# Forty-one unread products of the identity among the opening's instructions on TensorE

## The chip, the cores and the metric

One NeuronCore of a Trainium2 chip runs the kernel. The metric is device time in microseconds (us), from three runs of the kernel before: 505.88, 505.97 and 508.54, median 505.97. Lower is better.

TensorE multiplies and transposes (PE in the profile, its weight loads PEld), VectorE (DVE) and ScalarE (ACT) do elementwise work and read TensorE's results out of the accumulation memory PSUM, GpSimd (POOL) does elementwise work and issues transfers, SyncE (SP) only issues transfers. Each engine runs its own instructions strictly in the order of the program; semaphores hold one engine back until another has delivered.

## What is computed

Two layers in fp32. The first is a delta-rule attention with a state of 48 x 48 for each of 4 x 8 heads, over 768 steps:

```python
k_n = k / (np.linalg.norm(k, axis=-1, keepdims=True) + 1e-06)
state = np.zeros((B, H, D, D))
for t in range(S):
    y[:, :, t] = einsum('bhd,bhde->bhe', q[:, :, t], state)
    v_old = einsum('bhde,bhd->bhe', state, kt)
    state = state + bt[..., None, None] * einsum('bhd,bhe->bhde', kt, vt - v_old)
```

The second takes its output as 3072 tokens of 384 numbers and applies a maxout network, with w1, w2 and w3 of 384 x 768 and w_out of 768 x 384:

```python
h = np.maximum(np.maximum(x @ w1, x @ w2), x @ w3)
return h @ w_out
```

## The kernel before

**Tiling.** The 768 steps are cut into 12 chunks of 64. A chunk has two units, one for each pair of batch entries, so there are 24 units. Two chunks (512 tokens) form a group, and there are six groups. Inside a chunk the recurrence is turned into matrix products. That needs the Gram matrices of keys with keys and keys with queries, and the inverse of a triangular matrix for each head. The inverse is found by forward substitution on VectorE (`solve`, from line 507), all heads at once. Then small products on TensorE join the halves of the inverse and make the updates `u`, the outputs `y` and the state `st`.

**Order.** The whole order is written out by hand, under a manual schedule: the program's order is each engine's order. The last part of the kernel (from line 1276) is this order. First comes the opening, straight-line code for the first chunks; then the six groups of the second layer, `ffn(0)` to `ffn(5)`, with the recurrence of the next group laid between their products.

**The opening, line by line of what TensorE gets.** `turn(n, (0,))` transposes unit n's keys by four products with the identity (tile `p_t`, line 338) and copies them out; `turn(n, (1,))` does the same for queries. `keys(n)` and `gram(n, ...)` make Gram matrices (`p_g`, line 415) and copy them out (lines 426 and 432). `some(solving, n)` issues n steps of the forward substitution on VectorE (lines 561 and 565). At the end of group 0's substitution the result is transposed on VectorE (line 573) and placed in `ut` by copies of VectorE and ScalarE (line 505). Next, for chunk 0, come `halves_z` (`p_e`, line 685), `halves_u` (`p_f`, line 696), `join_z` (`p_z`, line 713), `join_u` (`p_j`, line 726), `new` (`p_u`, line 771), `to_y` (`p_y`, line 813) and `to_x` (`p_x`, line 832). Each is a batch of 32 small products, in two halves where it is chunk 0, and a copy follows on ScalarE or VectorE that the next batch needs. `to_x` is six transposes, which fill the tile `xt` that the second layer reads.

Between them stand `some(conv, 1)`, one step of the conversion of the second layer's weights (three instructions on ScalarE, lines 247 to 249, one on VectorE, line 259, one on GpSimd, line 263), and `fetch`, which loads a piece of them. `solve(1)` starts the second group's inverse; its substitution runs on VectorE in the stretch after the opening.

`ffn(0)` then starts with products `p_h` (line 1224) of `xt` with converted weights. Between its first steps lie, in this order, chunk 1's `halves_z`, chunk 0's state update (`p_s`, line 794, added to `st` on VectorE at line 801), chunk 1's `halves_u`, and `old_k` (`p_k`, line 743, subtracted from `v_t` on VectorE at line 755).

**The product in question.** `busy(n, of)` at line 1290 already exists. It multiplies the 128 x 128 identity by `of`, n times, into a PSUM tile `p_w` that nothing reads. The tile takes one of the two slots named `ffn`, which in the opening nothing else uses. Before, it is called once, at line 1309, ahead of the first transposes of keys. A product in fp32 is two matmul instructions in the trace; a transpose is one.

Of the kernel before, what the change touches and what calls it, by code (L numbers as in the profile page):

```python
# [23 lines left out]
def kernel(  # L24
# [76 lines left out]
    ident = const.tile([128, 128], FP32, name="ident")  # L101
# [208 lines left out]
    def first_norms():  # L310
        nc.vector.transpose(out=nrm_0.rearrange("p c g h -> p (c g h)"), in_=bl_0[0])
# [7 lines left out]
    def by_par(t):  # L319
        return t.rearrange("p (j two) x -> p two j x", two=2)  # L320

    def turn(n, parts=(0, 1), copy=nc.scalar.copy):

        if n not in kqts:
            if n == 6:
                kqts[n] = work.tile([128, KT, TOK], FP32, name="xt").rearrange(
                    "p k t -> p (k t)"
                )[:, 0 : NP * 4 * C].rearrange(
                    "p (j b i t) -> p j b i t", b=2, i=2, t=C
                )  # L330
            else:
                kqts[n] = work.tile([128, NP, 2, 2, C], FP32, name="kqt", bufs=6)
        kqt = kqts[n]
        p_t = ps_two("p_t")
        for i in parts:
            src = (kpad[place(n)], qpad[n % NQ])[i]
            for j in range(NP):
                nc.tensor.transpose(
                    p_t[:, i, j * 128 : (j + 1) * 128],
                    src[:, 2 * j : 2 * j + 2],  # L340
                    ident,
                )
        some = slice(parts[0], parts[-1] + 1)
        copy(  # L344
            kqt.rearrange("p j b i t -> p i (j b) t")[:, some],
            p_t.rearrange("p i (x t) -> p i x t", t=C)[:, some],
        )
# [50 lines left out]
    def masked(t, of, engine=nc.vector):  # L398
        engine.tensor_tensor(  # L399
            out=by_par(t), in0=of,  # L400
            in1=mask[:, None, None, :].to_broadcast([128, 2, NP, C]), op=ALU.mult,
        )

    def gram(n, parts=(0, 1), queues=one_queue, copy=nc.scalar.copy, later=False):
        kqt, g = kqts[n], n % 2
        p_g = ps_two("p_g")

        whole = len(parts) == 2 and not g
        for j in range(NP):
            for par in range(2):  # L410
                for bb in range(2):
                    kq = kqt[dims(par), j, bb ^ g]
                    for i in (0,) if whole else parts:
                        c0 = j * 128 + i * C
                        nc.tensor.matmul(  # L415
                            p_g[
                                rows(bb ^ (g * i)), par, c0 : c0 + C * (1 + whole)
                            ],
                            kq[:, 0],
                            kq if whole else kq[:, i],  # L420
                        )
        p_v = p_g.rearrange("p two (j i t) -> p two j i t", j=NP, i=2)
        if 1 in parts:
            pt = pts[n] = square("pt")
            if later:
                copy(by_par(pt), p_v[:, :, :, 1])
            else:
                masked(pt, p_v[:, :, :, 1])
        if 0 not in parts:
            return  # L430
        at = ats[n] = square("at")
        copy(by_par(at), p_v[:, :, :, 0])  # L432
        if queues:
            to_dram(n, queues)
# [192 lines left out]
    def turn_t1(c):  # L627

        t, u_t = t1[c % NU], ut[c % NU]
        nc.vector.transpose(out=t[:, 0], in_=u_t[:, 0, :, 0:BL])  # L630
        for bb in range(2):
            nc.vector.transpose(
                out=t[block(1 - bb), 1], in_=u_t[block(bb), 1, :, 0:BL]
            )
# [41 lines left out]
    def halves_z(c):  # L676
        if c > 1:
            halves_t(c)
        at = [ats[2 * c + g] for g in range(2)]
        second = ut[c % NU].rearrange("p g h (f two x) -> p g h f two x", two=2, x=HB)  # L680
        for hs, p_v, copy in heads_of(c, "p_e", BL):
            for i, h in enumerate(hs):
                for bb, g in TILES:
                    r = rows(bb)
                    nc.tensor.matmul(
                        p_v[rows(bb ^ g), g, i], at[g][r, h], second[r, g, h, :, 1]
                    )
            copy(zs[c % NU][:, :, span(hs)], p_v)

    def halves_u(c):  # L690
        t, z = fine.pop(c), zs[c % NU]
        for hs, p_v, negate in negated_of(c, "p_f", BL):
            for i, h in enumerate(hs):
                for bb, g in TILES:
                    r = rows(bb ^ g)
                    nc.tensor.matmul(p_v[bb][rows(bb), g, i], t[g][r, h], z[r, g, h])
            for f in (0, 1):
                for bb in range(2):
                    r = block(bb, f, HB)
                    negate[bb](  # L700
                        ut[c % NU][r, :, span(hs), BL * f + HB : BL * (f + 1)],
                        p_v[bb][r, :, :, HB * f : HB * (f + 1)],
                        -1.0,
                    )

    def join_z(c):
        at = [ats.pop(2 * c + g) for g in range(2)]
        z, second = zs[c % NU], ut[c % NU][:, :, :, BL:C]
        for hs, p_v, _ in heads_of(c, "p_z", BL):
            for i, h in enumerate(hs):  # L710
                for bb, g in TILES:
                    r = block(bb, 1)
                    nc.tensor.matmul(
                        p_v[block(bb ^ g), g, i], at[g][r, h, 0:BL], second[r, g, h]
                    )
            for bb in range(2):
                nc.scalar.copy(z[block(bb), :, span(hs)], p_v[block(bb)])

    def join_u(c):
        z, t = zs[c % NU], t1[c % NU]  # L720
        u12 = ut[c % NU][:, :, :, BL:C]
        for hs, p_v, negate in negated_of(c, "p_j", BL):
            for i, h in enumerate(hs):
                for bb, g in TILES:
                    r = block(bb ^ g)
                    nc.tensor.matmul(p_v[bb][block(bb), g, i], t[r, g, h], z[r, g, h])  # L726
            for bb in range(2):
                negate[bb](u12[block(bb), :, span(hs)], p_v[bb][block(bb)], -1.0)
# [36 lines left out]
    def new(c):  # L765
        rhs = rhss.pop(c)
        u = us[c] = both("u", D, 2)
        for hs, p_v, copy in heads_of(c, "p_u", D):
            for i, h in enumerate(hs):
                for bb, g in TILES:  # L770
                    nc.tensor.matmul(  # L771
                        p_v[rows(bb ^ g), g, i],
                        ut[c % NU][rows(bb), g, h],
                        rhs[rows(bb), g, h],
                    )
            copy(u[:, :, span(hs)], p_v)
        if c + NU < 2 * FINE:
            for bb in range(2):
                corner = ut[c % NU][block(bb), :, :, BL:C]
                zero = kpad[0][block(bb), None, 0:1, D : D + 1]  # L780
                nc.scalar.copy(corner, zero.to_broadcast(corner.shape))
# [494 lines left out]
    def some(gen, n):  # L1276
        for _ in range(n):
            if next(gen, gen) is gen:
                break
# [10 lines left out]
    def busy(n, of):  # L1290
        p_w = ps_ffn([128, TOK], "p_w")[:, 0 : of.shape[1]]
        for _ in range(n):
            nc.tensor.matmul(p_w, ident, of)

    def keys(n, queues=one_queue, copy=nc.scalar.copy):
        gram(n, (0,), queues, copy)
# [30 lines left out]
    some(solving, 1)  # L1327
    keys(4)
    keys(5)
    turn(6, (0,))  # L1330
    turn(0, (1,))
    load_q(3, (nc.gpsimd, nc.gpsimd))
    load_beta()
    keys(6)
    gram(0, (1,), None, later=True)
    turn(7, (0,))
    turn(1, (1,))
    keys(7)
    turn(2, (1,))
    gram(1, (1,), None, later=True)  # L1340
    turn(3, (1,))
    some(conv, 1)
    gram(2, (1,), None, later=True)
    gram(3, (1,), None, later=True)
    some(solving, HB + 1)
    halves_t(0)
    halves_z(0)
    first_norms()
    some(conv, 1)
    placed(1, 0)  # L1350
# [3 lines left out]
    for _ in range(2):  # L1354
        fetch(nc.gpsimd)
    halves_u(0)
    turn_t1(0)
    join_z(0)
    masked(pts[0], by_par(pts[0]))
    placed(1, 2)  # L1360
    join_u(0)
    masked(pts[1], by_par(pts[1]))
    old_k(0)
    old_q(0)
    new(0)
    some(conv, 1)
    fetch(nc.gpsimd)
    load_v(1, nc.gpsimd)
    placed(1, 3)
    to_y(0)  # L1370
    halves_t(1)
    solving = solve(1)
    some(solving, 1)
    to_x(0)
    some(conv, 1)


# [177 lines left out]
```

## Time and profile before

| view | value |
|---|---|
| median of three runs | 505.97 us (505.88 to 508.54) |
| the profiled execution's span | 505.2 us |
| TensorE busy | 484.0 us, 96% of the span |
| VectorE busy | 361.1 us, 71% |
| ScalarE busy | 169.4 us, 34% |
| GpSimd busy | 187.1 us, 37% |
| mean granted TensorE clock | 0.968 |

The span runs from the first instruction to the last in one profiled execution. Busy time is the sum of recorded instruction times; matmuls are pipelined, so consecutive records overlap and a busy TensorE is not one at its peak. The granted clock is given as a share of full speed: 1.00 is full, 0.50 is half. A wait shows as idle time before an instruction, with the instruction that ended it.

### The profile page before, as it was taken

Reading aid. Unit: us, or ns where it says so; the run is one execution under the profiler, and the core shown is the slowest. Engines: PE = TensorE matmul, PEld = TensorE weight load, DVE = VectorE, ACT = ScalarE, POOL = GpSimd, SP = SyncE. Lnnn points to the kernel's source line nnn. Section 1 sums busy time; section 2 is a strip of 40 time slices with the busy share of each in tenths; the row PEclk is TensorE's granted clock in tenths of the full one; section 3 lists DMA queues with packets and bytes.
Section 4 is the critical chain, followed back from the end, with each engine's and each line's share of the span. In section 5 each row is a group of like instructions: output and inputs, shape, how many; then the busy total and the mean of one; then the engine's idle time right before and its main releaser. Section 6 shows DMA issues by size and latency. Waiting matters only on the chain.

```text
span 505.2 us, 18676 instructions
## 1 busy us (share of the span) xinstructions
PE 484.0 (96%) x8064; PEld 338.0 (67%) x8064; DVE 361.1 (71%) x835; ACT 169.4 (34%) x320; POOL 187.1 (37%) x311
## 2 busy tenths in 40 slices
PE   7678989999999999999999999999999999999996
PEld 6467767855566555565565565555797457998895
DVE  5888799787996441799652999565998874468753
ACT  5585664885422142210152200242201032212210
POOL 7434472793391935770395880501000020000000
PEclk9855899999999999999999999999999999999999
DMA  8937869864045934544584652744224230340002
GB/s 114 205 50 214 195 142 160 198 181 137 3 120 134 191 72 77 146 119 117 112 156 104 158 137 74 149 72 96 64 54 90 47 86 15 85 94 1 0 18 47
DMA packets 109121, 53.50 MB, mean 106 GB/s; under 512 B 92208, under 2 KB 102864, under 8 KB 109040
## 3 DMA queue, kind: packets, MB, share of 16 engines
q1 hardware_dynamic: 97280, 31.78, 31.0%
q0 software_dynamic: 9216, 19.85, 16.5%
q8 instruction: 63, 1.03, 0.9%
q10 hardware_dynamic: 2544, 0.69, 0.8%
q14 instruction: 18, 0.15, 0.1%
HBM read 39.17 MB, written 13.11 MB: 103 GB/s over the span
## 4 chain that ended last, share of the span: by engine, by line
PE 76%; DVE 11%; ACT 4%; DMA 3%; SPq 3%; issue 2%; POOL 0%; DVEq 0%; ACTq 0%; POOLq 0%
PE p_h L1224 28%; PE p_o L985 13%; PE p_o L1262 12%; PE p_c L1163 5%; DVE tmp L561 3%; PE p_g L415 2%; PE p_m L905 2%; PE p_u L771 2%; PE p_k L743 2%; DVE y_p L565 2%; DMA kmore<-in_k_dram 2%; PE p_y L813 2%; PE p_s L794 2%; PE p_q L743 1%; PE p_j L726 1%
## 5 line engine op out<-in xcount | busy, mean ns | idle before, releaser
L1224 PE MATMUL p_h<-xt,w_sb 128*128 128x512 f32 (+1 forms) x450 | 186.8, 558 | 0.6 <-ACT xt L839 0.6
L1224 PEld LDWEIGHTS p_h<-xt,w_sb 128*128 128x128 f32 x450 | 82.4, 193 | 69.2 <-issue 61.6
L1238 DVE TENSOR_TENSOR h<-h,p_h 128x512 f32<-128x512 f32 (+1 forms) x42 | 25.5, 607 | 46.8 <-PE p_h L1224 46.3
L565 DVE TENSOR_TENSOR y_bl<-y_bl,tmp 128x31 f32<-128x31 f32 (+20 forms) x139 | 50.4, 363 | 4.8
L561 DVE TENSOR_TENSOR tmp<-x_bl,y_bl 128x31 f32<-128x31 f32 (+20 forms) x139 | 48.8, 351 | 3.9
L1262 PE MATMUL p_o<-wo_sb,h 128*128 128x384 f32 x144 | 48.9, 490 | 0.0
L373 POOL DMA_DIRECT2D turned<-in_q_dram x72 | 39.3, 554 | 4.6 <-POOL turned L368 3.1
L1262 PEld LDWEIGHTS p_o<-wo_sb,h 128*128 128x128 f32 x144 | 26.7, 190 | 17.2
L1234 ACT ACTIVATE h<-p_h 128x512 f32<-128x512 f32 x24 | 14.3, 597 | 69.2 <-PE p_h L1224 69.2
L263 POOL TENSOR_TENSOR w_sb<-mant,up 128x384 int32<-128x384 int32 x18 | 19.0, 1054 | 39.5 <-DVE mant L259 37.8
L415 PEld LDWEIGHTS p_g<-kqt 48*64 48x64 f32 x1216 | 24.5, 142 | 9.2 <-issue 6.3
L415 PE MATMUL p_g<-kqt 48*64 48x64 f32 (+1 forms) x1216 | 27.7, 241 | 0.9 <-ACT kqt L344 0.8
L1268 ACT COPY o_sb<-p_o 128x384 f32<-128x384 f32 x12 | 5.8, 479 | 62.6 <-PE p_o L1262 56.5
L801 DVE TENSOR_TENSOR st<-st,p_s 48x768 f32<-48x768 f32 (+1 forms) x18 | 17.1, 949 | 12.7 <-PE p_s L794 12.4
L399 DVE TENSOR_TENSOR pt<-p_g,mask 128x512 f32<-128x512 f32 x20 | 13.8, 690 | 17.0 <-PE p_g L415 16.9
L598 POOL DMA_DIRECT2D ut<-y_d x4 | 2.6, 653 | 60.6 <-DMA y_d<-y_bl 60.6
L148 POOL DMA_DIRECT2D v_t<-in_v_dram x14 | 11.6, 832 | 35.3 <-PE p_u L771 35.3
L368 POOL MEMSET turned<- 128x96 f32 x18 | 3.3, 191 | 49.4 <-DVE kqt L389 49.4
L771 PEld LDWEIGHTS p_u<-v_t,ut 64*64 64x64 f32 x768 | 13.5, 141 | 8.4 <-issue 7.3
L432 ACT COPY at<-p_g 128x512 f32<-128x512 f32 x22 | 12.8, 585 | 17.4 <-DVE pt L399 15.4
L373 POOL DMA_DIRECT2D turned<-in_k_dram x32 | 17.5, 556 | 1.2 <-POOL turned L368 1.2
L1163 PE MATMUL p_c<-xt,w_sb 128*128 128x256 f32 x72 | 17.7, 379 | 0.0
(239 smaller groups left out, 907.3 us busy)
## 6 DMA issues: line engine op xcount, KB each, us to landing
w_bits<-in_moe_w_dram SPq DMA_DIRECT2D x9, 384.0 KB, 6.2
w_bits<-in_moe_w_dram POOLq DMA_DIRECT2D x9, 384.0 KB, 5.7
turned<-in_q_dram POOLq DMA_DIRECT2D x72, 48.0 KB, 2.8
out_dram<-o_sb SPq DMA_DIRECT2D x36, 96.0 KB, 2.3
y_x<-y SPq DMA_DIRECT2D x32, 96.0 KB, 3.0
qall<-y_x SPq DMA_DIRECT2D x32, 96.0 KB, 2.8
v_t<-in_v_dram POOLq DMA_DIRECT2D x14, 192.0 KB, 5.0
at_d<-at SPq DMA_DIRECT2D x72, 32.0 KB, 3.0
```

What stands on the lines that cost most here:

```text
L263: nc.gpsimd.tensor_tensor(out=dst.bitcast(I32), in0=mant_v.bitcast(I32), in1=up_v, op=ALU.add)
L373: (queue, nc.gpsimd)[i].dma_start(out=t[p0 : p0 + 32, bb, at : at + NP * 2 * D].rearrange("p (j x) -> p j x", j=NP), in_=(k, q)[i][2 * bb ...
L415: nc.tensor.matmul(p_g[rows(bb ^ (g * i)), par, c0 : c0 + C * (1 + whole)], kq[:, 0], kq if whole else kq[:, i],)
L561: nc.vector.tensor_tensor(out=t_v, in0=row.to_broadcast(t_v.shape), in1=column.to_broadcast(t_v.shape), op=ALU.mult,)
L565: nc.vector.tensor_tensor(out=rest, in0=rest, in1=t_v, op=ALU.subtract)
L771: nc.tensor.matmul(p_v[rows(bb ^ g), g, i], ut[c % NU][rows(bb), g, h], rhs[rows(bb), g, h],)
L801: nc.vector.tensor_tensor(out=s_v[r], in0=s_v[r], in1=p_s[r, :, 0 : H * D], op=ALU.add)
L985: nc.tensor.matmul(to[:, g], a[j][:, 128 * g : 128 * (g + 1)], b[j], start=(start and g == j == 0), stop=(stop and g == 1 and j == len(a) ...
L1163: nc.tensor.matmul(to, w[stays], moves, start=(n == 0), stop=(n == len(terms) - 1))
L1224: nc.tensor.matmul(p_h, w_sb[i][:, t, f * 128 : (f + 1) * 128], xt[:, t, lo : lo + w], start=(t == 0), stop=(t == KT - 1),)
L1238: nc.vector.tensor_tensor(out=h, in0=h, in1=p_h, op=ALU.max)
L1262: nc.tensor.matmul(p_o, stays, moves, start=(n == 0), stop=(n == len(terms) - 1))
```

## The change

At twelve places of the opening a call of `busy` with the identity is put in: 2, 3, 3, 6, 6, 2, 4, 3, 4, 3, 3 and 2 products, 41 in all. Nothing is removed or moved, and no transfer is added. In the program's order these places are: before the turn of unit 6's keys; before the turn of unit 7's keys; before the queries of units 2 and 3; after the last Gram matrix of group 0, ahead of `halves_z(0)`; and after `halves_z`, `halves_u`, `join_z`, `join_u`, `new`, `to_y` and `to_x` of chunk 0.

```diff
     keys(5)
+    busy(2, ident)
     turn(6, (0,))
...
     gram(0, (1,), None, later=True)
+    busy(3, ident)
     turn(7, (0,))
     turn(1, (1,))
     keys(7)
+    busy(3, ident)
     turn(2, (1,))
     gram(1, (1,), None, later=True)
+    busy(6, ident)
     turn(3, (1,))
     some(conv, 1)
     gram(2, (1,), None, later=True)
     gram(3, (1,), None, later=True)
+    busy(6, ident)
     some(solving, HB + 1)
     halves_t(0)
     halves_z(0)
+    busy(2, ident)
     first_norms()
...
     halves_u(0)
+    busy(4, ident)
     turn_t1(0)
     join_z(0)
+    busy(3, ident)
     masked(pts[0], by_par(pts[0]))
     placed(1, 2)
     join_u(0)
+    busy(4, ident)
     masked(pts[1], by_par(pts[1]))
     old_k(0)
     old_q(0)
     new(0)
+    busy(3, ident)
...
     to_y(0)
+    busy(3, ident)
     halves_t(1)
     solving = solve(1)
     some(solving, 1)
     to_x(0)
+    busy(2, ident)
     some(conv, 1)
```

## The prediction

> **What bounds the kernel now.** I looked first at the busy time by long stretches (columns: stretch and length; busy us and instructions of PE, PEld, DVE, ACT, POOL; granted clock; DMA share; GB/s).
>
> ```profile
> 30.00:55.00 25.00, 22.51 (x618) 19.46 (x622) 19.43 (x46) 15.16 (x37) 14.00 (x15) 0.54 0.58 147
> 55.00:90.00 35.00, 31.62 (x710) 26.14 (x701) 32.05 (x83) 22.08 (x42) 15.88 (x20) 1.00 0.89 165
> 100.00:500.00 400.00, 399.85 (x6113) 267.75 (x6112) 279.10 (x639) 106.30 (x196) 134.98 (x232) 1.00 0.41 93
> ```
>
> From 100 us on TensorE never waits: what reaches that point earlier ends earlier. From 55 to 90 VectorE sets the pace (32.05 of 35 us, the substitution of `solve(1)`). Before that the clock stands at 0.54. So I cut the opening finely, along the steps at which the clock changed. Slices of 0.1 us put these at 18.97, 22.38, 25.79 and 53.07 us: steps of 3.41, 3.41 and 27.28, which is 8 times 3.41.
>
> ```profile
> 12.15:15.56 3.41, 2.17 (x72) 1.88 (x72) 2.84 (x6) 2.06 (x6) 2.21 (x3) 1.00 0.93 166
> 15.56:18.97 3.41, 2.14 (x72) 1.60 (x70) 2.77 (x11) 2.62 (x5) 1.94 (x3) 1.00 1.25 217
> 18.97:22.38 3.41, 3.41 (x56) 2.63 (x60) 3.03 (x11) 1.53 (x3) 2.27 (x5) 0.50 1.36 224
> 22.38:25.79 3.41, 0.87 (x32) 0.70 (x24) 3.02 (x12) 0.81 (x2) 0.00 (x0) 1.00 1.10 199
> 46.25:49.66 3.41, 3.41 (x76) 2.58 (x77) 3.12 (x10) 0.43 (x2) 0.00 (x0) 0.50 0.89 197
> 49.66:53.07 3.41, 3.41 (x72) 3.05 (x68) 1.47 (x4) 2.14 (x4) 3.19 (x3) 0.50 0.84 149
> ```
>
> Each clock holds for such a slot and answers to the slot before: 2.14 us of work lost it, 2.17 kept it, a full slot (3.41) won it back at 22.38, 0.87 lost it again, and from 25.79 it stayed at half until 53.07. One full slot, from 46.25, did not win it; it holds the small products `p_e` in half its length.
>
> Third, the timeline of TensorE, for what half clock costs and where it waits (start, us, engine, line, operation, count, idle before).
>
> ```profile
> 25.34 0.67 PE L338 MATMUL p_t<-ident,qall 128*128 128x128 f32 x4 [2.54 <-DMA qall<-in_q_dram]
> 30.13 0.43 PE L685 MATMUL p_e<-ut,at 64*64 64x32 f32 x6 [2.21 <-ACT ut L505]
> 34.88 1.24 PE L713 MATMUL p_z<-ut,at 32*32 32x32 f32 x64 [0.47 <-ACT ut L700]
> 42.83 1.52 PE L832 MATMUL p_x<-ident,y 128*128 128x128 f32 x6 [0.77 <-ACT y_p L525]
> 44.92 2.93 PE L1224 MATMUL p_h<-xt,w_sb 128*128 128x256 f32 x6 [0.57 <-ACT xt L839]
> 55.71 1.56 PE L1224 MATMUL p_h<-xt,w_sb 128*128 128x256 f32 x6
> 57.20 0.75 PE L713 MATMUL p_z<-ut,at 32*32 32x32 f32 x64
> ```
>
> The same six `p_h` take 2.93 us at half clock and 1.56 at full; `p_z` 1.24 and 0.75.
>
> **The change, part by part.** It adds 82 matmul instructions with their weight loads and nothing else: no transfer, no queue of SP or POOL, no reader of the tile. The `ffn` slots have no other user before `p_h`, and a later write is TensorE's own, so no wait is added.
>
> *Price.* The twelve `p_w` of the existing call start 2.01 and the next `p_t` starts at 4.73: 0.227 us each, the half-clock price. At full clock the nearest rows are four transposes in 0.43 to 0.49 us start to start (0.108 to 0.122 each). I take the upper, 0.245 a product: 41 cost 10.0 us at full clock, and 18.6 at half. Below nothing is possible only through the clock, which is the next point.
>
> *The first 20 (2+3+3+6+6), before `halves_z` at 30.13.* They cost 4.9 us at full clock. TensorE waits 0.84, 0.30, 0.25, 0.71, 2.54 and 2.21 us in this stretch, 6.85 in all, and what it delivers is not late: `halves_z` waits for ScalarE's copies into `ut` (two, 29.03 to 30.73), which follow VectorE's substitution (until 28.42) and ScalarE's own conversion and mask copies (26.5 to 29.0). I charge nothing; without that cover it would be the 4.9.
>
> *What they do to the clock.* Slot 15.56 goes from 2.14 to about 2.9 us: the drop at 18.97 goes away. Then turns and Gram matrices run at full clock, the six products ahead of unit 3's queries end near 23.2, and TensorE still waits for the query load until 25.34. Slot 22.38 holds 0.9 + 0.45 us, so I expect the drop at 25.79. Next come 2.0 us of `p_g` until 27.9 and then products without a gap: slot 25.79 is full, and the clock is back at 29.20 instead of 53.07. The six then end near 29.95 (three at 0.45, three at 0.245), ahead of 30.13.
>
> *The last 21 (2+4+3+4+3+3+2), between 30 and 45.* At full clock 5.1 us. The seven batches around them, `p_e` to `p_x`, have 12.3 us of busy rows at half clock; half of that, 6.1, is freed. It does not show as a plain difference, because the copies between set the pace. I walked it, each engine in its order, full-clock batches at half their rows:
> - `p_f` cannot start before 32.3, where VectorE's transposes into `t` end (32.33). ScalarE's conversion starts 0.5 earlier, since `p_e` ends sooner, and with it its copies into `ut`. `p_z` could start at 34.4; four products behind `p_f` hold it to 34.5 (was 34.88).
> - `p_j` at 36.0 (was 36.45; VectorE's `t1` ends then, and three products just fit). `p_u` at 37.8: four products hold it, its operand is there at 37.2 (was 38.10). Its second half waits for VectorE's copy, 38.6, and ends 39.2 (was 40.2).
> - `p_y` ends 41.05 (was 42.05), `p_x` starts 41.8 (was 42.83), and ScalarE, which first clears `y_p` (1.0 us), ends the copies into `xt` at 43.5. `p_h` starts there: 1.4 gained.
> - VectorE's transposes and norm for `solve(1)` move by 1.05 with `y`, to the end of their scaling at 48.2. TensorE meanwhile needs 1.4 + 1.0 + 1.05 us for `p_h`, `p_e`, `p_s`, until 47.0 instead of 51.4. So the update of `st` waits for VectorE and starts at 48.55 (was 51.51): 3.0 gained.
> - `p_k` ends at 50.6, but VectorE has two steps, a mantissa shift and a maximum first: `v_t` at line 755 starts at 51.05 instead of 55.91. 4.86 gained.
>
> From there VectorE runs almost without a gap to 89 us, and behind it TensorE without one; the 4.86 are carried. I take off 0.25 for one more handover like the one ahead of `p_u` ([0.24 <-issue]). Sum: 505.2 - 4.6 = 500.6 of span. The run shown is 0.77 above its span (505.97 - 505.2), so **501.4 us**.
>
> The Trainium skill, "TensorE: Matmul & The Clock Gate", Part 1, says the clock is decided on a free-running window of 3413 ns, and that one busy window releases it. The slots above agree on the length; the full slot from 46.25 at half clock does not agree that being busy is enough. By the page's rule slot 25.79 releases the clock, as I take it; by the row it may not.
>
> **The rivals.**
> - *The clock comes back later*, at 36.02, since `p_g` in slot 25.79 fills no better than `p_e` in slot 46.25. Then two products cost 0.9 before `p_f` and four push `p_z` to 36.65; `p_j` starts at 38.0, `p_x` at 43.4 and `p_h` at 44.75, level with before. The rest of `ffn(0)`'s first steps is at full clock, and `v_t` starts at 52.7: 3.2 gained, 502.8. For it: the row at 46.25. Against: `p_g` filled 1.5 us of slot 18.97, which won the clock.
> - *Weights come too late for the faster start.* GpSimd issues a weight piece at 54.65; it lands 5.7 later, at 60.35, and ScalarE takes it at 63.98. ScalarE wants it 4.9 earlier, while the issue, behind two other GpSimd steps, moves by only 2.0: 0.7 to spare. If it takes the 9.1 us of the piece issued at 72.78, it is 2.7 late, which gives 501.4 + 2.7 = 504.1. Against: the four pieces issued between 46 and 55 take 4.7 to 6.2.
> - *Slower: the clock stays low while the products are paid at 0.453.* The place is the chain from `p_e` to `p_x`. Two push `p_f` by 1.1, four more `p_z` by 2.4, three `p_j` by 3.3, four `p_u` by 4.9, three `p_y` by 6.5 and three `p_x` by 7.0. If the clock comes back near 43, `p_h` to `p_k` give 3.9 back: 509. If only at 53, 513. It decides from the point where neither slot 25.79 nor the two after it count as full enough; for it speaks again 46.25, against it that identity products load the whole array.
> - *Pure cost: the clock is not set by how full TensorE is, and the last 21 are only added.* 5.1 us less the waits that they can fill there (0.22, 0.47, 0.24, 0.77, 0.57: 2.3) is 2.8 us: 508.8. Against: the 0.50 rows follow emptier slots at 18.97 and 25.79. The Trainium skill's same page, "Why this matters for your kernels", ties a drop to idle gaps of about 3 us; TensorE's longest here is 2.54, so by that rule nothing would have dropped, and it did.
> - *The clock rises and nothing comes of it*, because something between 56 and 100 us is tied to a load, as the query load that ends TensorE's 1.01 us wait at 85.84: about 505.5. Against: that load is issued behind TensorE's own transposes, so it moves too.
>
> **How the numbers follow.** Forecast 0.53, later clock 0.20, late weights 0.12, low clock 0.07, pure cost 0.02, nothing 0.06. VectorE's idle time from 30 to 55.91 (0.40, 0.35, 0.47, 0.33, 1.89, 0.31, 1.61: 5.4) caps the gain at `v_t`, which gives 500.6; a further 1 us of TensorE's waits after 56 may close, so the low end is 499.6. The high end takes in the later clock, the late weights and the lower edge of no effect: 505.6. The forecast's own range is 500.3 to 502.5. A measurement here tells 0.5%, 2.5 us, from nothing. Faster by more: the forecast and nearly all of the later clock, 0.72. Within: late weights, no effect and the rest, 0.18. Slower: 0.10.
>
> **What would show it.** Clock 1.00 at 18.97 to 22.38; 0.50 at most for 25.79 to 29.20; 1.00 from then on. The first `p_h` near 43.5 with six in about 1.5 us; `v_t` at line 755 near 51; busy rows from 56 on the same, only shifted. I am wrong if the clock is low in 29 to 45, if TensorE's waits between 30 and 45 do not shrink, or if a weight piece ends ScalarE's waits after 50.

## The result and the profile after

The changed kernel takes 513.24 us (median; 511.64 to 516.16) against 505.93 for the kernel before, four runs of each. The ratio on record is 1.0125, 95% interval 1.0088 to 1.0162 (the quotient of the two medians is 1.0145). It is slower, clear of noise, while the mean granted clock rose from 0.968 to 0.991. The profiled execution has a span of 509.9 us (505.2 before). It is the shortest of the four, so the traces account for 4.7 us of the 7.3 between the medians; the rest lies in executions without a trace.

The same three long stretches, now of the changed kernel (columns as before):

```profile
30.00:55.00 25.00, 22.54 (x744) 19.45 (x745) 22.57 (x50) 17.24 (x42) 14.97 (x15) 1.00 0.66 159
55.00:90.00 35.00, 30.08 (x605) 25.32 (x605) 28.44 (x77) 19.11 (x35) 14.30 (x18) 0.90 0.86 155
100.00:500.00 400.00, 396.35 (x6085) 263.84 (x6084) 276.13 (x638) 105.92 (x196) 134.52 (x232) 1.00 0.41 92
```

The clock in the first row is what was wanted, 1.00 instead of 0.54. The second row is what was not: VectorE works 28.44 of 35 us (32.05 before), TensorE 30.08, and the clock is back at 0.90. In the third, TensorE has lost 3.5 us of 400 that it had not lost before. The timeline of TensorE in the changed kernel shows the places:

```profile
34.49 0.77 PE L713 MATMUL p_z<-ut,at 32*32 32x32 f32 x64
...
44.32 1.56 PE L1224 MATMUL p_h<-xt,w_sb 128*128 128x256 f32 x6 [0.70 <-ACT xt L839]
...
51.50 0.37 PE L696 MATMUL p_f<-z,t 64*64 64x32 f32 x12 [1.24 <-issue]
...
55.66 0.38 PE L713 MATMUL p_z<-ut,at 32*32 32x32 f32 x22 [0.79 <-issue]
...
63.30 1.09 PE L743 MATMUL p_q<-st,kqt 48*64 48x48 f32 x29 [4.26 <-issue]
64.32 2.93 PE L1224 MATMUL p_h<-xt,w_sb 128*128 128x256 f32 x6
...
106.75 0.72 PE L713 MATMUL p_z<-ut,at 32*32 32x32 f32 x60 [0.85 <-DMA ut<-y_d]
...
119.85 0.91 PE L794 MATMUL p_s<-u,kmore 64*64 64x48 f32 x45 [0.56 <-issue]
...
130.45 0.20 PE L743 MATMUL p_q<-st,xt 48*64 48x48 f32 x1 [0.94 <-issue]
...
181.33 0.87 PE L713 MATMUL p_z<-ut,at 32*32 32x32 f32 x65 [0.44 <-issue]
...
336.02 0.26 PE L713 MATMUL p_z<-ut,at 32*32 32x32 f32 x8 [0.87 <-issue]
```

"Issue" means that the engine waited for nothing that the profile shows: no semaphore held it. TensorE stops in the middle of a batch of small products, the longest time 4.26 us, behind the 35th of 64 `p_q`. That leaves 1.64 and 0.92 us of work in two slots of 3.41 us, so the clock is at half from 60.81 to 67.64, and the next six `p_h` cost 2.93 us. I matched the instructions of both kernels one by one. The changed one is 2.91 us ahead at `v_t` and 3.44 behind at `p_u` of chunk 1. It is almost level at 86 us (0.12 behind), because the kernel before waits there for 1.01, 0.74 and 1.02 us and the changed one does not. Then it loses 1.1 at 106.75, where it waits for the load of `ut`, and 3.6 at the four issue waits, to 4.80 at 336. The wait for `ut` is put down to a load, not to issue, and its cause stays open: two kernels with a filled piece, wide100 and realigned_fetch_b below, have it too (1.50 and 1.23 us).

**What the stops have in common.** Between those at 51.50, 55.66 and 63.30 the trace has 127 matmuls each time (12 + 3 + 1 + 63 + 6 + 42, and 22 + 6 + 64 + 35): 254 instructions with their weight loads. One queue of the profile, q8, carries pieces of 16 KB. From the stop at 51.50 to the one at 336.02, 38 of these landed and 4829 matmuls ran, 127.1 to a piece. The queue's line on the page of the kernel before (packets, MB, share of 16 engines):

```profile
q8 instruction: 63, 1.03, 0.9%
```

The same line on the page of the changed kernel:

```profile
q8 instruction: 64, 1.05, 0.9%
```

Before, TensorE has 8064 matmuls and as many weight loads, 63.5 times 254 instructions, and 63 pieces; after, 164 instructions more, 64.1 times, and 64 pieces. So I read this queue as TensorE's own instructions, some 256 to a piece, of which about two are neither matmuls nor weight loads. The 256 itself is tested below: 256 added instructions bring the stops back to the same places. The pieces also fit in time: of the waits on issue of 0.4 us or more behind 24 us, 52 in the 14 traces of this document, every one ends 1.25 to 1.73 us after a piece of q8 has landed. Of the transfers of the changed kernel, these are the queues from 55 to 60 us, and the last line is that of q8 from 60 to 65 (packets, MB, share of 16 engines):

```profile
q1 hardware_dynamic: 2060, 0.73, 74.2%
q0 software_dynamic: 112, 0.39, 26.9%
...
q8 instruction: 2, 0.03, 3.0%
```

In this stretch no piece comes while data fills the DMA engines. Full engines alone do not hold a piece back, though: the kernel before took one at 62.88, and from 60 to 65 its q1 had 98.3%. In the trace's list of transfers the pieces around the long stop run from 53.3 to 54.3 and from 60.3 to 61.8. TensorE goes on at 55.66 and 63.30, some 1.4 us after each. From going on at 55.66 TensorE needs 3.4 us for the next 127 matmuls at full clock, most of them small; from there to going on with the piece after them took 7.6 us.

### The profile page after: what moved, and what is told of

The parts are those of the page before. It is cut to its first block, busy times and chain, and to the rows that moved or that the text cites. A ratio compares the mean times of both kernels' runs of the same rounds, so it can differ in the third digit from the quotient of the medians.

```text
span 509.9 us, 18841 instructions
## 1 busy us (share of the span) xinstructions
PE 487.3 (96%) x8146; PEld 341.3 (67%) x8146; DVE 360.7 (71%) x835; ACT 168.9 (33%) x320; POOL 187.0 (37%) x311
## 4 chain that ended last, share of the span: by engine, by line
PE 83%; DMA 5%; DVE 4%; issue 3%; SPq 2%; ACT 1%; POOL 1%; POOLq 0%; DVEq 0%
PE p_h L1224 32%; PE p_o L985 12%; PE p_o L1262 12%; PE p_c L1163 5%; PE p_g L415 3%; PE p_u L771 2%; PE p_m L905 2%; PE p_y L813 2%; PE p_k L743 2%; PE p_q L743 2%; PE p_s L794 2%; DMA kmore<-in_k_dram 2%; PE p_j L726 2%; PE p_z L713 1%; DVE tmp L561 1%
## 5 line engine op out<-in xcount | busy, mean ns | idle before, releaser
L565 DVE TENSOR_TENSOR y_bl<-y_bl,tmp 128x31 f32<-128x31 f32 (+20 forms) x139 | 48.5, 349 | 4.8
L415 PEld LDWEIGHTS p_g<-kqt 48*64 48x64 f32 x1216 | 23.4, 134 | 10.2 <-issue 7.4
L129 POOL DMA_DIRECT2D kpad<-in_k_dram x24 | 16.4, 691 | 2.9 <-PE p_s L794 2.9
```

Of the source, the lines that this page charges most:

```text
L415: nc.tensor.matmul(p_g[rows(bb ^ (g * i)), par, c0 : c0 + C * (1 + whole)], kq[:, 0], kq if whole else kq[:, i],)
L565: nc.vector.tensor_tensor(out=rest, in0=rest, in1=t_v, op=ALU.subtract)
```

## The experiments

Theory A: the 164 added instructions moved all later piece ends, into batches of small products. Theory B: the products' own time on the chain, or a faster TensorE as such. All ratios are those on record, to the kernel before in the same series, since it took 505.9 to 509.3 us in different ones; the quotients of the medians differ from them by up to 0.33%. A tiny product is 32 x 32 by 32 x 32, two matmuls and two weight loads of hardly any work:

```diff
+    def tiny(n):
+        p_w = ps_ffn([128, TOK], "p_w")
+        for i in range(n):
+            r = slice(64 * (i % 2), 64 * (i % 2) + 32)
+            nc.tensor.matmul(p_w[r, 0:32], ident[r, r], ident[r, r])
```

**Fill the last piece up (realigned).** The change, and 23 tiny products: 82 + 46 = 128 matmuls.

```diff
     gram(3, (1,), None, later=True)
     busy(6, ident)
+    tiny(23)
     some(solving, HB + 1)
```

> All 41 products as in the change, and 23 tiny products (32 x 32 by 32 x 32, 46 matmuls and 46 weight loads) behind the second group of six. Theory A (TensorE's instructions arrive in pieces of 16 KB, 256 instructions, and the 164 added ones moved the piece ends into batches of small products): with 256 added instructions every piece after 45 us ends at the same instruction as in the kernel before, the issue waits of 4.26, 0.85, 0.56, 0.94, 0.44 and 0.87 us go away, the gain of about 2.9 us at the subtraction of old values stays: 502 to 504 us. Theory B (the products themselves on the chain, or a faster TensorE as such, starve it): the tiny ones change nothing, 511 to 516 us.

Measured: 507.78 us, ratio 1.0006 (0.9968 to 1.0044). The loss is gone, by adding still more instructions. Theory B, which said 511 to 516, falls. Stops remain between 50 and 66 us (0.57, 1.36, 1.18 and 0.99), and TensorE is ahead at 86 all the same; what went away are the stops behind 86. But 502 to 504 was missed: the gain did not last either (below).

**The instructions without the work (tiny41).** `busy(n, ident)` is `tiny(n)` at all twelve places.

> The 41 products at the same twelve places, but 32 x 32 by 32 x 32: the same number of instructions, hardly any work, so no help for the clock. Theory A: the piece ends lie where they lie in the changed kernel, so issue waits appear between 100 and 340 us as there (about 3.5 us together), and the clock is low until about 53 us as before: 508 to 512 us. Theory B: no more than the tiny products' own time, 505.5 to 507 us.

Measured: 514.67, ratio 1.0155 (1.0116 to 1.0195), above the range given, and no better than the real products. Its timeline of TensorE has stops at the same matmuls as the changed kernel's:

```profile
119.61 0.90 PE L794 MATMUL p_s<-u,kmore 64*64 64x48 f32 x45 [1.09 <-issue]
...
130.81 0.20 PE L743 MATMUL p_q<-st,xt 48*64 48x48 f32 x1 [1.53 <-issue]
```

In this trace the two stops cost 3.3 us, and half clock from 131.66 to 135.07 behind the second one 1.5 more. A slowdown as large as that of the change comes with the added instructions alone, without their work. (The clock was back at 42.91 already, not at about 53 as expected.)

**One whole piece at one place (one64).**

```diff
     gram(3, (1,), None, later=True)
+    tiny(64)
     some(solving, HB + 1)
```

> The kernel before with 64 tiny products at one place, after the last Gram matrix of group 0, where TensorE waits 2.2 us: 256 added instructions, one whole piece. Theory A: all piece ends after it fall as before, 505.5 to 507 us. If it is the number of added instructions as such that hurts, not where pieces end, it is slower than the 41: over 510 us.

Measured: 508.39, ratio 1.0032 (1.0005 to 1.0059), where the kernel before took 507.23. More instructions than the change adds, and a quarter of its loss, though 1.4 us above the bound given: the trace has an issue wait of 1.58 us inside the 128 tiny matmuls themselves, and `p_e` starts 1.4 us late. At the end its trace is 2.9 us behind that of the kernel before, so not all of its loss is explained.

**A fifth of a piece (one14).** The same place, `tiny(14)`.

> The kernel before with 14 tiny products at one place: 56 added instructions and no work. Theory A: piece ends move by 56 instructions; some other small products are hit, so the time moves by up to some us either way, 504 to 512 us, by issue waits that a listing of TensorE's waits after 86 us shows. Theory B: 505.5 to 508 us, no wait on issue after 86 us.

Measured: 511.91, ratio 1.0102 (1.0054 to 1.0151). Fourteen products of next to no work cost 1%. The stops in its timeline of TensorE, at other matmuls than above:

```profile
115.57 0.45 PE L771 MATMUL p_u<-v_t,ut 64*64 64x48 f32 x16 [1.40 <-issue]
...
180.53 0.31 PE L713 MATMUL p_z<-ut,at 32*32 32x32 f32 x11 [0.74 <-issue]
```

**The same work in fewer instructions (wide, wide100).** 14 products with up to 512 columns: 28 matmuls, so the ends of one14. The second adds `tiny(50)` to fill the piece.

```diff
+    def wide(n):
+        of = kpad[0].rearrange("p h d -> p (h d)")[:, 0 : 128 * n]
+        nc.tensor.matmul(ps_ffn([128, TOK], "p_w")[:, 0 : 128 * n], ident, of)
```

> The same twelve places and the same columns streamed, but as 14 wide products (up to 512 columns of a tile of keys) in place of 41 narrow ones: 28 added matmuls and 28 weight loads instead of 82 and 82. Theory A (piece ends of 256 instructions): the ends lie 56 instructions further, not 164, so the issue waits fall at other places than in the changed kernel; how long they are together is what one14 shows without the products. With the clock's help as in the changed kernel it should be 1 to 3 us faster than one14. Theory B (the products' time on the chain): the same time in the chain, so as slow as the changed kernel, 511 to 516 us.

> The wide products and 50 tiny ones behind the fifth call: 256 added instructions, all piece ends after 45 us as in the kernel before. Theory A: no issue wait after 86 us; as the run with 41 narrow products and 23 tiny ones, 504 to 508 us, a little less if the batches of the opening get their instructions sooner. Theory B: 511 to 516 us.

Measured: wide 513.48, ratio 1.0124 (1.0086 to 1.0162); wide100 509.27, ratio 1.0030 (0.9995 to 1.0066). The first has the stop of one14 at 115.90 (1.41 us), but is not faster than it: by time alone it can't be told from theory B, only by its waits. The second again takes most of the loss away, though it lies above the 504 to 508 given. Its trace has no issue wait over 0.31 us behind 86; the wait for the load of `ut` (1.50 us at 104.89) cost the clock one slot.

**Which products hold the clock (first20, first20_b, last21).** The first five calls and `tiny(44)`, twice, or the last seven and `tiny(43)`; 128 matmuls in all.

> Only the first five calls (20 products), and 44 tiny products behind them: 256 added instructions, so piece ends after 45 us as before; the last seven calls (21 products) are left out. If the last 21 are needed to hold the clock, it falls to half between 30 and 45 us and v_t (line 755) starts later than 53 us, by 1 to 2 us: 506 to 508 us. If the clock holds without them, the 21 were only time on the chain: v_t near 52, 503 to 506 us.

> The kernel of first20 once more, in more rounds. If the 2.3 us that its trace gains by 86 us last to the end in most executions, it is faster than the kernel before by 0.2 to 0.6%. If they are mostly lost at a load, as in realigned at the load of blocks for the third inverse, it is the same within 0.2%.

> Only the last seven calls (21 products), and 43 tiny products ahead of them: 256 added instructions. If the first 20 are needed to bring the clock up before 30 us, it stays at half until products fill slots later, and the products are paid at half speed on the chain: p_h starts 1 to 2 us later than 44.9, 507 to 510 us. If the 21 alone bring it up soon, as realigned, 505 to 508 us.

Measured: 0.9988 (0.9954 to 1.0022), 1.0009 (0.9976 to 1.0041) and 1.0033 (1.0002 to 1.0063). In first20 the clock fell at 36.93 to 43.76 and `v_t` started at 54.75: the last 21 are needed for the clock, but no gain in time by them is shown (0.9988 without them, 1.0006 with them in realigned). In last21 the clock was at half from 25.34 to 38.99, and the products were paid at that price on the chain. The timeline of TensorE in last21:

```profile
34.03 1.22 PE L1293 MATMUL p_w<-ident 128*128 128x128 f32 x4
35.18 1.93 PE L696 MATMUL p_f<-z,t 64*64 64x32 f32 x64
37.04 2.07 PE L1293 MATMUL p_w<-ident 128*128 128x128 f32 x8
39.04 0.75 PE L713 MATMUL p_z<-ut,at 32*32 32x32 f32 x64
```

`p_z` comes 4.2 us later than before. Of this, 1.6 is the tiny products, behind which `p_e` starts at 31.74 instead of 30.13; the other 2.6 is the slower rival's mechanism at work, which had 2.4 there. `p_h` starts 3.2 us late, more than the 1 to 2 expected. The profiled execution of first20_b shows one reason why single times spread: there the clock first came up at 15.0 us (5 to 7 in the other traces), so the first transposes and Gram matrices ran at half speed. VectorE's first transpose into `x_bl` (line 480) started 3.0 us late, at 15.34, and at `p_y`, behind more work at half clock, the lag was 4.9 us.

**Where the realigned kernel loses its gain (realigned_fetch, realigned_fetch_b, fetch_only).** In the trace of realigned TensorE is 2.63 us ahead at 86 and 0.45 at 131, with no issue wait of more than 0.15 us between. The timeline of realigned, first SyncE's issue of a load, then ScalarE, then TensorE:

```profile
107.10 0.35 SPq L492 DMA_DIRECT2D x_bl<-at_d  x1
...
114.96 0.27 ACT L270 ACTIVATE root_bl<-x_bl 128x32 f32<-128x32 f32 x1 [1.53 <-DMA x_bl<-at_d]
...
123.43 0.33 PE L743 MATMUL p_k<-st,xt 48*64 48x48 f32 x8 [0.86 <-DVE st L801]
...
130.21 1.15 PE L771 MATMUL p_u<-v_t,ut 64*64 64x48 f32 x64 [1.00 <-DVE v_t L755]
```

The load of blocks for the third inverse is issued 2 us earlier than before (109.13) and is ready only 0.4 earlier (`root_bl` at 115.41). VectorE then waits for it, and TensorE for VectorE. The edit moves three of five weight loads out of its way:

```diff
-    FETCHED = {8: 1, 12: 1, 13: 1, 14: 1, 18: 2, 19: 2, 20: 1, 21: 1}
+    FETCHED = {8: 1, 12: 1, 13: 1, 14: 1, 18: 2, 20: 2, 21: 1, 22: 1}
```

> The kernel of realigned with three of the five weight loads of steps 18 to 21 of ffn(0) issued one step later, away from the load of blocks that took 7.84 us there. If that load was slowed by these, it lands near 112 instead of 115, VectorE's third substitution starts some 2 us earlier, TensorE's waits on VectorE at 123 and 130 us go away, and the gain of 2.6 us at 86 us lasts: 503 to 505 us in the trace's execution, 0.3% under realigned. If not, as realigned.

> The kernel of realigned_fetch once more. If its 0.27% is real, the interval again lies mostly under 1, between 0.993 and 1.000; if it was the draw of executions, the ratio is 1.000 within 0.003.

> The kernel before with nothing but the three weight loads issued one step later. There the load of blocks was not waited for, so the move alone should give nothing: a ratio of 1.000 within 0.003. If it gives the 0.27% by itself, the products have no part in the gain of realigned_fetch.

Measured: 506.33, ratio 0.9973 (0.9939 to 1.0006); again 507.37, ratio 0.9955 (0.9925 to 0.9985); and the move alone 509.68, ratio 1.0018 (0.9990 to 1.0046). In the first series' timeline ScalarE's wait for that load is nearly gone:

```profile
113.20 0.26 ACT L270 ACTIVATE root_bl<-x_bl 128x32 f32<-128x32 f32 x1 [0.25 <-DMA x_bl<-at_d]
```

TensorE's wait for `v_t` remained (1.1 us), and 2.1 us stay to the end. So the products, the filled piece and the moved loads together beat both kernels, by 0.45% in the second series, whose interval clears 1; the first leaves it open. In the second series' trace TensorE is only 1.2 us ahead at 86, another load (`ut` from `y_d`, 1.23 us) takes this back, and it ends 0.5 behind the trace of the kernel before. So how much lasts depends on the execution.

## Why the prediction was wrong, step by step

- *First 20 products hidden:* right. `p_e` started at 29.51 (30.13 before).
- *Clock:* right in direction, too careful in size. The drop at 18.97 went away (in realigned, with the same products, it came, at 18.81, so that is not sure in every execution); the one at 25.79, which I expected, did not come, because the queries of unit 3 were there at 23.90 and TensorE did not wait for them.
- *Walk through the last 21:* `p_z` 34.49 (34.5 forecast), `p_j` 36.05 (36.0), `p_u` 38.12 (37.8), `p_x` 42.25 (41.8), `p_h` 44.32 (43.5, so 0.6 gained instead of 1.4), `st` 48.96 (48.55). The mechanism holds, the gain at `p_h` was over-sized.
- *`v_t` at 51.05:* 53.00. Here the failed step begins: TensorE stopped for 1.24 us inside `p_f`.
- **The step that failed:** "It adds 82 matmul instructions with their weight loads and nothing else: no transfer". The instructions are themselves brought by transfers. I priced each product by its time on the array and gave it no price for its place in the stream. The cost is not the 164 instructions but where the later piece ends fall: tiny41 pays it without the work (1.0155), realigned does the work without paying it (1.0006).
- *"the 4.86 are carried":* wrong twice. In the changed kernel the gain was lost at 63.30; with the piece filled it was lost at the load of `x_bl`. My last rival (a load between 56 and 100 that does not move) had that mechanism, one load too early, and at 0.06.
- *The end of the sum:* 0.25 for one more handover stands against stops of 1.24, 0.79 and 4.26 us. The 0.77 between run and span seems to compare two executions, since every run with a span on record lies 1.6 us or more above it. That changes the level by about 1 us, not the sign.
- *The slower rival* had the sign, and its 513 is the measured time by luck, since its mechanism did not act here: the clock was 1.00 throughout the chain. Pure cost (508.8) had the sign too, and its premise fell: the clock did follow how full TensorE was. No rival named instruction supply, although a wait on issue stood in the profile before ([1.01 <-issue] at a `p_u`, 65.65 us), and I took such waits for small handovers.

The Trainium skill, "TensorE: Matmul & The Clock Gate", "Why this matters for your kernels", advises to keep TensorE busy for 4 us at a stretch to have the full clock. The trace agrees on the clock (0.54 to 1.00 from 30 to 55 us) and not on the time, which is 1.25% longer, since the filling is itself made of instructions.

What stays open: why the piece of 60.3 us started so late. Data transfers filled the DMA engines then, but no run took that traffic away. That q8 belongs to TensorE rests on its count of pieces, on the spacing of the stops and on their ends just behind a piece, not on a label. All traces are single executions; those of the changed kernel, tiny41, one14 and wide are each the shortest of four runs, and so show only part of the loss.

## What to carry to other kernels

Filler instructions were not free in this tightly ordered program, even where the engine idled: they shifted where every later piece of its instruction stream ends. Before judging such an edit, add the same number of instructions without work, and fill up to a whole piece; if the time moves with the count, the edit itself has not been measured yet. Look at waits on "issue" inside batches of short instructions first, and then at which load now comes last.

## What was not expected of the hardware

- TensorE's instructions came in pieces of 16 KB, some 256 to a piece, as far as the counts and the stops show it. 28 tiny matmuls in the wrong number cost 1.0%, 128 cost 0.3%.
- A stop on issue of 4.26 us was long enough to cost the clock too: half speed for 6.8 us.
- The clock's first rise differed between executions of the same opening, 5 to 7 us in most traces and 15 us in one, where VectorE's transpose at line 480 came 3.0 us late.
